# Third-stage products reordered, sums and stores of h moved forward, the first raw weights loaded by GpSimd's queue

## The chip, the cores and the metric

The kernel runs on one core of a Trainium2 chip. A core has five engines that run their own instruction streams and meet at semaphores: TensorE (PE, and PEld for its weight loads), VectorE (DVE), ScalarE (ACT), GpSimd (POOL) and SyncE (SP). DMA transfers are issued by SP's and GpSimd's queues here. The metric is the time of one execution on the device in microseconds (us).

## The reference

Sigmoid attention, then a "max of three" layer, then a layer with PReLU, all in float32:

```python
scores = scale * q @ k.T - log(S)          # 4 x 12 heads, S = 448, width 64
x = (1 / (1 + exp(-scores))) @ v           # -> 1792 tokens x 768
h = maximum(maximum(x @ w1, x @ w2), x @ w3)   # 768 x 768 each
x = h @ w_out                              # 768 x 768
h2 = x @ w_in                              # 768 x 2048
g = maximum(h2, 0) + alpha * minimum(h2, 0)
return g @ w_out2                          # 2048 x 768
```

## The kernel before

**Products.** Every matrix product behind attention is done by seven products for a 2 x 2 block (Strassen's scheme). A *unit* `u` is a pair of 128-wide column blocks of a weight matrix; for each unit there are seven products `k` = 0..6 for each of two halves `g` of the tokens. A product is nine matmuls of 128 x 448 columns: three slices of the contraction, and three for each, since a float32 operand is cut into a high half `h` (a cast on ScalarE, L277) and a low half `l` (source minus high half, on VectorE, L281), and low x high, high x low and high x high are added up.

**Banks.** `product(u, k, g)` (L831) writes three PSUM banks: k = 0 starts `X`, and ScalarE copies it to `V` (L850), to which k = 1 adds; k = 2 starts `W`; k = 3 and 4 add to `X`, and after each ScalarE copies `X` out (L865); k = 5 finishes `X`, k = 6 finishes `W`. The eviction (`evict`, L786) adds the copies to `W` on VectorE (`tensor_op`, L288). A product that adds to `X` while the copy of `X` still runs has to wait for it, and k = 1 waits for the copy to `V`.

**Stages.** Attention (0 to 138 us): scores L542, values L563, with q and k loaded by SP (L523), v by GpSimd (L531). Units 0 to 8 make h: three units, for w1, w2 and w3, for each of three column pairs, with the maximum on VectorE (`mx`). Behind the third unit `h_store` (L757) makes the sums that the next layer's seven products need (T = B12 - B11, then B22 - T and so on, into the same tiles) and GpSimd stores them to `hd` (L767); `reload` (L885) brings them back and cuts them. The *third stage* is h @ w_out: units 100 to 105, with g the half and weights `cf` from `cd` (`left_loads`, L942). Units 9 to 16 make the PReLU layer, behind which `ff3` follows (to the end).

**Weights.** A raw word `z` (384 KB) is loaded to `wr` by `load_half` (L132, four buffers; 112 words) on SP; `word_ops` (L230) unpacks it (two ScalarE passes, three VectorE instructions: L249, L250, L258); `unit_ops` (L314) adds and subtracts words (`wu`, `wt`) and cuts the seven left operands `f{u}_{k}`, from words 0 and 1 for k = 0 and 1, from all four for k = 2, 3 and 6. For w_out the operands are stored (L351) for the third stage; the words of units 9 and 10 are stored (`words_via`) and loaded as `wb`.

**Order.** All this is put by a planner into the programs while TensorE's products are written out by hand: `op(engine, columns, fn, *deps, gate, soon, lag)` registers a piece of work; each `advance()` behind a product emits what is ready and what fits a budget of columns, the `soon` ones first; `lag=n` holds an op back by n further steps behind what it depends on; `need()` forces out what a product is about to read. Each engine then works in the order in which its instructions were emitted, and so waits at the first that is not ready. The third stage's order is the loop behind `units(0, L, ...)`: for each of six units k = 0 to 6. L is 8, HK is 3, CU is 100, ND0 is 9.

## Time and profile before

| | us |
|---|---|
| median of three runs (955.11 to 958.52) | 958.07 |
| the profiled execution | 953.27 |
| its span in the trace | 951.5 |
| TensorE busy in the span | 873.8 |
| VectorE, ScalarE, GpSimd busy | 654.7, 525.8, 140.6 |

The mean granted TensorE clock over the span is 0.974 of full speed. The shares are averages over stages of different kinds. Where TensorE is the engine that is almost always busy, one looks at its pauses: an instruction's row carries, in brackets, the idle time before it and the instruction that ended it.

### The profile page before, as it was taken

Reading aid. Unit: us, or ns where it says so; the run is one execution under the profiler, and the core shown is the slowest. Engines: PE = TensorE matmul, PEld = TensorE weight load, DVE = VectorE, ACT = ScalarE, POOL = GpSimd, SP = SyncE. Lnnn points to the kernel's source line nnn. Section 1 sums busy time; section 2 is a strip of 40 time slices with the busy share of each in tenths; the row PEclk is TensorE's granted clock in tenths of the full one; section 3 lists DMA queues with packets and bytes.
Section 4 is the critical chain, followed back from the end, with each engine's and each line's share of the span. In section 5 each row is a group of like instructions: output and inputs, shape, how many; then the busy total and the mean of one; then the engine's idle time right before and its main releaser. Section 6 shows DMA issues by size and latency. Waiting matters only on the chain.

```text
span 951.5 us, 14131 instructions
## 1 busy us (share of the span) xinstructions
PE 873.8 (92%) x4878; PEld 742.0 (78%) x4878; DVE 654.7 (69%) x1289; ACT 525.8 (55%) x1021; POOL 140.6 (15%) x260
## 2 busy tenths in 40 slices
PE   9999997799699879988886789989999999999998
PEld 4466446698589778877775679888899999999997
DVE  1766766578588768777535459877886868787741
ACT  6877885444355536454424457765665755354530
POOL 1333000002210221320000013122222100000110
PEclk9999999899899979999998989999999999999999
DMA  7899520246544747697530126664544699834511
GB/s 241 293 306 308 161 72 6 85 143 206 174 139 143 230 150 221 240 352 223 178 112 26 47 72 197 205 223 143 174 147 165 230 348 374 301 106 152 175 50 48
DMA packets 78632, 170.46 MB, mean 179 GB/s; under 512 B 11120, under 2 KB 51856, under 8 KB 78560
## 3 DMA queue, kind: packets, MB, share of 16 engines
q1 hardware_dynamic: 61776, 111.10, 37.7%
q0 software_dynamic: 16496, 58.11, 16.4%
q8 instruction: 38, 0.62, 0.3%
q10 hardware_dynamic: 288, 0.34, 0.1%
q14 instruction: 34, 0.28, 0.1%
HBM read 123.12 MB, written 46.40 MB: 178 GB/s over the span
## 4 chain that ended last, share of the span: by engine, by line
PE 82%; DVE 7%; issue 4%; ACT 3%; DMA 3%; POOL 1%; SPq 0%; DVEq 0%; ACTq 0%; POOLq 0%
PE u_0X L670 15%; PE u_1X L670 13%; PE eW L670 9%; PE eX L670 9%; PE u_0W L670 8%; PE u_1W L670 6%; PE sc L542 6%; PE pav L563 6%; PE u_0V L670 4%; PE u_1V L670 3%; PE eV L670 3%; DMA qt<-in_q_dram 2%; ACT u L865 1%; DVE mx L288 1%; DVE wr L250 1%
## 5 line engine op out<-in xcount | busy, mean ns | idle before, releaser
L542 PE MATMUL sc<-qt,kt 64*64 64x448 f32 x672 | 97.6, 540 | 4.8 <-DMA qt<-in_q_dram 4.8
L563 PE MATMUL pav<-a,vt 64*64 64x448 f32 x672 | 95.9, 538 | 0.0
L550 ACT ACTIVATE a<-sc,bias_s 128x896 f32<-128x896 f32 x84 | 83.2, 1011 | 21.2 <-PE sc L542 20.2
L542 PEld LDWEIGHTS sc<-qt,kt 64*64 64x64 f32 x672 | 42.4, 134 | 36.4 <-issue 26.6
L258 DVE CUSTOM_DVE_ANT_0 wt<-wr,wt 128x768 uint16<-128x768 uint16 x112 | 62.6, 558 | 3.9
L250 DVE SCALAR_TENSOR_TENSOR wr<-wr 128x384 uint32<-128x384 uint32 x112 | 62.0, 553 | 3.4 <-ACT wr L242 3.1
L242 ACT ACTIVATE wr<-wr 128x384 uint32<-128x384 uint32 x112 | 61.6, 551 | 0.0
L865 ACT COPY u<-u_0X 128x448 f32<-128x448 f32 x40 | 21.3, 533 | 71.7 <-PE u_0X L670 71.7
L563 PEld LDWEIGHTS pav<-a,vt 64*64 64x64 f32 x672 | 40.1, 133 | 26.7 <-issue 20.8
L239 ACT ACTIVATE wt<-wr 128x384 f32<-128x384 f32 x100 | 55.3, 553 | 1.4 <-DMA wr<-in_weights_dram 1.4
L717 DVE SCALAR_TENSOR_TENSOR r<-n,nalpha,r 128x448 f32<-128x448 f32 x64 | 42.6, 681 | 16.9 <-ACT n L714 16.8
L750 POOL DMA_DIRECT2D gd<-r x48 | 26.3, 549 | 167.8 <-DVE r L717 148.8
L288 DVE TENSOR_TENSOR u<-u_1W,u 128x448 f32<-128x448 f32 x34 | 21.2, 624 | 37.9 <-ACT u L865 27.5
L288 DVE TENSOR_TENSOR u<-u_0W,u 128x448 f32<-128x448 f32 x34 | 21.2, 623 | 37.2 <-ACT u L865 34.6
L938 POOL DMA_DIRECT2D wd<-wt x32 | 17.8, 556 | 194.6 <-DVE wt L258 184.1
L865 ACT COPY u<-u_1X 128x448 f32<-128x448 f32 x40 | 21.3, 534 | 43.3 <-PE u_1X L670 43.3
L249 DVE TENSOR_SCALAR wt<-wt 128x384 uint32<-128x384 uint32 x112 | 39.8, 355 | 1.4 <-ACT wt L239 1.0
L578 DVE COPY x<-pav 128x448 f32<-128x448 f32 x12 | 7.5, 625 | 38.0 <-PE pav L563 38.0
L670 PE MATMUL u_0W<-x_2h,f_2l 128*128 128x448 f32 x27 | 12.1, 447 | 21.9 <-DVE f_2l L281 21.9
L850 ACT COPY u_0V<-u_0X 128x448 f32<-128x448 f32 x20 | 10.4, 518 | 38.1 <-PE u_0X L670 38.1
L670 PEld LDWEIGHTS u_0W<-x_2h,f_2l 128*128 128x128 f32 x27 | 5.8, 216 | 24.6 <-DVE f_2l L281 24.1
L1265 ACT COPY p<-eW 128x448 f32<-128x448 f32 x12 | 6.4, 534 | 32.9 <-PE eW L670 32.9
(813 smaller groups left out, 2828.1 us busy)
## 6 DMA issues: line engine op xcount, KB each, us to landing
wr<-in_weights_dram SPq DMA_DIRECT2D x112, 384.0 KB, 3.7
gl<-gd SPq DMA_DIRECT2D x79, 224.0 KB, 4.0
wl<-wd SPq DMA_DIRECT2D x64, 192.0 KB, 4.5
gd<-r POOLq DMA_DIRECT2D x48, 224.0 KB, 3.0
gl_T<-gdT SPq DMA_DIRECT2D x32, 224.0 KB, 5.3
hr<-hd POOLq DMA_DIRECT2D x28, 224.0 KB, 5.9
wd<-wt POOLq DMA_DIRECT2D x32, 192.0 KB, 3.9
kt<-in_k_dram SPq DMA_DIRECT2D x23, 224.0 KB, 4.8
```

What stands on the lines that cost most here:

```text
L239: nc.scalar.activation(st["T"].bitcast(F32), st["r"][:, :, 1].bitcast(F32), AF.Abs, scale=2.0**-112)
L242: nc.scalar.activation(st["r"][:, :, 0], st["r"][:, :, 0], AF.Copy, scale=2.0**-29)
L249: nc.vector.tensor_scalar(st["T"], st["T"], 3, None, ALU.logical_shift_left)
L250: nc.vector.scalar_tensor_tensor(out=st["r"][:, :, 0], in0=st["r"][:, :, 1], scalar=0x80000000, in1=st["r"][:, :, 0], op0=ALU.bitwise_and, ...
L258: nc.vector.tensor_tensor(out=st["T"], in0=st["r"][:, :, 0], in1=st["T"], op=ALU.add)
L288: nc.vector.tensor_tensor(out=out, in0=a, in1=b, op=op)
L542: nc.tensor.matmul(sc[g * KH : (g + 1) * KH, j, :S], keys[u, z][r, m * KH : (m + 1) * KH], queries[u, z][r], start=True, stop=True,)
L550: nc.scalar.activation(a, sc[:, :, :S], AF.Sigmoid, bias=bias_s, scale=scale)
L563: nc.tensor.matmul(pv[key][j * D : (j + 1) * D, :S], vts[u][r, m, j], a[r, j], start=start, stop=stop,)
L670: nc.tensor.matmul(ps[:, : rh.shape[-1]], lt, rh, start=(start and z == 0), stop=(stop and z == len(mms) - 1), skip_group_check=True,)
L717: nc.vector.scalar_tensor_tensor(out=s["r"], in0=s["n"], scalar=nalpha[:, f : f + 1], in1=s["r"], op0=ALU.mult, op1=ALU.add,)
L865: nc.scalar.copy(side[g, k], banks[X][:, :TW])
```

## The change

- **Attention.** Raw words z < 16 are loaded by GpSimd's queue instead of SP's. The first unit's words are registered with pair 4 instead of pair 7, behind a gate that waits until all w_out pieces are cut. The stores of those pieces come two steps later.
- **`h_store`.** Stores get `lag=2` and `soon`, the four sums get `soon` and lose their lag; so a store stands three steps or more behind its sum, an overwrite of T at the next step behind its store.
- **Reload.** The lag moves from the cut to the load (which has nothing that it depends on), and the tiles come in the order 0, 2, 3, 1, 4, 6, 5.
- **Third stage.** Each unit's products run in the order 0, 2, 3, 1, 4, then product 0 of the next unit, then 6 and 5; the copies are kept by unit so that two units can be open. The end of unit 8 is drawn together with it (its last two products stand behind the first two of unit 100), and product 0 of unit 9 stands in front of the last two of unit 105. `left_loads` follows this list.
- **Passage to unit 9.** Its words are registered at the second product of unit 104 instead of the start of unit 105, without a gate on the words; only the pieces 4 to 6 keep gates.

```diff
@@ -133,7 +133,8 @@
         if z >= NZ:
             return
         t = wpool.tile([P, HF, 2], U32, tag="wr", name=f"wr{z}", bufs=4)
-        nc.sync.dma_start(out=t.rearrange("p f t -> p (f t)"), in_=weights[z])
+        queue = nc.gpsimd if z < 16 else nc.sync
+        queue.dma_start(out=t.rearrange("p f t -> p (f t)"), in_=weights[z])
...
-                op("Q", 0, gone, op("Q", 0, put, o), lag=2)
+                op("Q", 0, gone, op("Q", 0, put, o, lag=2))
...
-                        unit_ops(-1 - r, zc[r], words=lambda z: word_ops(z, early=True), store=True)
+                        done += unit_ops(-1 - r, zc[r], words=lambda z: word_ops(z, early=True), store=True)
...
-                if (u, c) == (7, 0):
-                    unit_ops(0, zu[0])
+                if (u, c) == (4, 0):
+                    free_ws = lambda: all(o.step is not None for o in done)
+                    unit_ops(0, zu[0], words=lambda z: word_ops(z, gate=free_ws))
...
-                return op("Q", 0, store, *deps)
+                return op("Q", 0, store, *deps, lag=2, soon=True)
...
-            o1 = op("D", TW, t1)
+            o1 = op("D", TW, t1, soon=True)
             p1 = put(2, lambda: b["T"], o1)
-            o3 = op("D", TW, lambda: tensor_op(B12, B22, B12, ALU.subtract), o1)
+            o3 = op("D", TW, lambda: tensor_op(B12, B22, B12, ALU.subtract), o1, soon=True)
             put(4, lambda: B12, o3)
-            o2 = op("D", TW, lambda: tensor_op(b["T"], B22, b["T"], ALU.subtract), p1, lag=2)
+            o2 = op("D", TW, lambda: tensor_op(b["T"], B22, b["T"], ALU.subtract), p1, soon=True)
             put(3, lambda: b["T"], o2)
-            o4 = op("D", TW, lambda: tensor_op(B21, B21, b["T"], ALU.subtract), o2, o21, lag=2)
+            o4 = op("D", TW, lambda: tensor_op(B21, B21, b["T"], ALU.subtract), o2, o21, soon=True)
             held[g] = [o22, put(5, lambda: B21, o4)]
...
-            X, V, W = ((g, x) for x in "XVW")
+            X, V, W = ((u, g, x) for x in "XVW")
...
-            o = op("Q", 0, load, gate=lambda: homes_h(c, 3) and gate())
-            o = split_ops(
-                hf[g, c, r], make, lambda: st["x"], TW, o, gate=lambda: homes_h(c, 2), lag=2
-            )
+            o = op("Q", 0, load, gate=lambda: homes_h(c, 3) and gate(), lag=2)
+            o = split_ops(hf[g, c, r], make, lambda: st["x"], TW, o, gate=lambda: homes_h(c, 2))
...
-            for x in o:
+            for x in o[skip:]:
...
+            for n, (p, k) in enumerate(third):
+                f, d = wf[CU + p][k], cd[-1 - p % HK, k]
+                if n < 3:
+                    gate = lambda: all(o.step is not None for o in last) and (L, 0, 0) in made
+                elif n < 5:
+                    gate = lambda n=n: (L, (0, 2)[n - 3], 1) in made
+                else:
+                    gate = lambda x=third[n - 4]: (CU + x[0], x[1], x[0] // HK) in made
...
-                for c in range(7):
+                for c in inner:
...
+        inner = (0, 2, 3, 1, 4, 6, 5)
+        third = [(0, 0)]
+        for p in range(2 * HK):
+            third += [(p, k) for k in inner[1:5]] + [(p + 1, 0)] * (p < 2 * HK - 1) + [(p, k) for k in inner[5:]]
         first, seq = (0, 2, 1, 3, 4, 5, 6), (0, 2, 3, 4, 1, 5, 6)
         units(0, L, first, range(7), (
-            (0, 0), (0, 1), (2, 0), (1, 0), (3, 0), (1, 1), (4, 0), (2, 1), (5, 0), (6, 0), (3, 1),
-            (4, 1), (5, 1),
+            (0, 0), (0, 1), (2, 0), (3, 0), (2, 1), (1, 0), (4, 0), (3, 1), (6, 0), (5, 0), (1, 1), (4, 1),
         ))
 
-        back = {}
-        for n in range(2 * HK):
-            g, r = n // HK, n % HK
-            u = CU + n
+        z0, z1 = zu[ND0], zu[ND0 + 1]
+        extra = {0: (L, 6, 1), 1: (L, 5, 1), len(third) - 3: (ND0, first[0], 0)}
+        for n, (p, k) in enumerate(third):
+            u = CU + p
             if n == 0:
-                for c in range(4):
+                for c in inner[:4]:
                     for x in range(HK - 1):
-                        reload(1, c, x, lambda: (L, 6, 1) in made)
-            elif n == HK - 1:
-                for c in range(4, 7):
+                        reload(1, c, x, lambda: (L, 5, 1) in made)
+            elif (p, k) == (HK - 1, inner[1]):
+                for c in inner[4:]:
                     for x in range(HK - 1):
                         reload(1, c, x, lambda: True)
-            elif n == 2 * HK - 1:
-                z, at = zu[ND0], {0: 0, 1: 0, 2: 3, 3: 4, 4: 5, 5: 6, 6: 6}
+            elif (p, k) == (2 * HK - 2, inner[1]):
+                at = {4: 1, 5: 4, 6: 6}
                 cuts = unit_ops(
-                    ND0, z, [lambda k=k: (u, at[k], 1) in made for k in range(7)],
-                    words=lambda x: via[0][x - z](lambda: (u - 1, 5, 1) in made),
+                    ND0, z0, [lambda k=k: k not in at or (CU + 2 * HK - 1, at[k], 1) in made for k in range(7)],
+                    words=lambda x: via[0][x - z0](None),
                 )
-            for k in range(7):
-                product(u, k, g)
-                advance(STEP)
-                if (n, k) == (0, 0):
-                    step(L, 6, 1)
-        z1 = zu[ND0 + 1]
+            product(u, k, p // HK)
+            advance(STEP)
+            if n in extra:
+                step(*extra[n])
         unit_ops(
             ND0 + 1, z1, None,
             words=lambda x: via[1][x - z1](lambda: all(o.step is not None for o in cuts)),
@@ -1022,7 +1021,7 @@
 
         units(ND0, ND1 - 1, first, seq, (
             (0, 1), (0, 0), (2, 1), (3, 1), (2, 0), (4, 1), (1, 1), (3, 0), (5, 1), (6, 1),
-        ))
+        ), 1)
         swap()
 
         advance(STEP)

```

Where the diff leaves open what the planner makes of it, the programs' orders show it. First VectorE in unit 3, where the first `h_store` falls: `h00_t` and `h10_t` are the two halves' T, `mx` the maxima, `f3_1l` and `f3_2l` the low halves that products 1 and 2 of unit 3 read; the lines L249, L250, L258 (after: L250, L251, L259) are one word. Before:

```order
L258 ISA wt36_2468<-wr36_2395,wt36_2468 128x768
L288 TENSOR_TENSOR wu3_2544<-wt34_2430,wt35_2448 128x384
L288 TENSOR_TENSOR h00_t_2562<-mx0_0_1_1879,mx0_0_0_1739 128x448
L288 TENSOR_TENSOR h00_t_2562<-mx0_1_1_1802,h00_t_2562 128x448
L288 TENSOR_TENSOR mx0_1_0_1842<-mx0_1_0_1842,h00_t_2562 128x448
L288 TENSOR_TENSOR h10_t_2583<-mx0_0_3_2018,mx0_0_2_1859 128x448
L288 TENSOR_TENSOR h10_t_2583<-mx0_1_3_1942,h10_t_2583 128x448
L288 TENSOR_TENSOR mx0_1_2_1981<-mx0_1_2_1981,h10_t_2583 128x448
L281 TENSOR_TENSOR f3_2l_2593<-wu3_2544,f3_2h_2572 128x384
L288 TENSOR_TENSOR wt34_2430<-wt32_2356,wt34_2430 128x384
```

After:

```order
L289 TENSOR_TENSOR h00_t_2494<-mx0_0_1_1874,mx0_0_0_1733 128x448
L289 TENSOR_TENSOR mx0_0_1_1874<-mx0_1_1_1796,mx0_0_1_1874 128x448
L289 TENSOR_TENSOR h10_t_2517<-mx0_0_3_2012,mx0_0_2_1856 128x448
L289 TENSOR_TENSOR mx0_0_3_2012<-mx0_1_3_1936,mx0_0_3_2012 128x448
L282 TENSOR_TENSOR f3_1l_2536<-wt33_2408,f3_1h_2478 128x384
L250 TENSOR_SCALAR wt34_2426<-wt34_2426 128x384
L251 SCALAR_TENSOR_TENSOR wr34_2342<-wr34_2342 128x384
L259 ISA wt34_2426<-wr34_2342,wt34_2426 128x768
L289 TENSOR_TENSOR h00_t_2494<-mx0_1_1_1796,h00_t_2494 128x448
L289 TENSOR_TENSOR mx0_1_0_1836<-mx0_1_0_1836,h00_t_2494 128x448
L289 TENSOR_TENSOR h10_t_2517<-mx0_1_3_1936,h10_t_2517 128x448
L289 TENSOR_TENSOR mx0_1_2_1978<-mx0_1_2_1978,h10_t_2517 128x448
```

The first sums of both T now stand ahead of `f3_1l`, with other sums, `f3_1l` and a word between each of them and the instruction that overwrites it. Behind these rows another word, `wu3` and `f3_2l` follow, so the overwrites still stand ahead of `f3_2l`.

Second TensorE in the third stage, unit 101, at the end of product 3 (weights `cf1_3`). Before:

```order
L670 MATMUL u101_0X_4385<-h0_31h_4099,cf1_30_4375 128x448
L670 MATMUL u101_0X_4385<-h0_3h_4223,cf1_31_4377 128x448
L670 MATMUL u101_0X_4385<-h0_3l_4255,cf1_30_4375 128x448
L670 MATMUL u101_0X_4385<-h0_3h_4223,cf1_30_4375 128x448
L670 MATMUL u101_0X_4385<-h0_40h_4101,cf1_41_4399 128x448
L670 MATMUL u101_0X_4385<-h0_40l_4285,cf1_40_4397 128x448
L670 MATMUL u101_0X_4385<-h0_41h_4117,cf1_41_4399 128x448
```

After:

```order
L672 MATMUL u101_0X_4322<-h0_31h_4086,cf1_30_4336 128x448
L672 MATMUL u101_0X_4322<-h0_3h_4211,cf1_31_4338 128x448
L672 MATMUL u101_0X_4322<-h0_3l_4231,cf1_30_4336 128x448
L672 MATMUL u101_0X_4322<-h0_3h_4211,cf1_30_4336 128x448
L672 MATMUL u101_0V_4332<-h0_10h_4104,cf1_11_4360 128x448
L672 MATMUL u101_0V_4332<-h0_10l_4277,cf1_10_4358 128x448
L672 MATMUL u101_0V_4332<-h0_11h_4106,cf1_11_4360 128x448
```

Behind the product that ends in `X`, before, the next one adds to `X` again; after, it adds to `V`.

Third ScalarE at the start of unit 9: casts of the weight pieces `f9_k` and the copy of unit 9's product 0 to bank V (`u9_0V`). Before:

```order
L277 CAST f9_0h_5118<-wb68_4987 128x384
L850 COPY u9_0V_5132<-u9_0X_5122 128x448
L277 CAST f9_1h_5138<-wb69_4989 128x384
L277 CAST f9_2h_5140<-wu9_5059 128x384
L277 CAST f9_5h_5157<-wb71_4993 128x384
L277 CAST y12_0h_5159<-y12_11_5004 128x448
L277 CAST y12_1h_5161<-y12_21_5089 128x448
L713 ACTIVATE r0_0_5174<-u9_0V_5132 128x448
L714 ACTIVATE n0_0_5175<-u9_0V_5132 128x448
L277 CAST y11_3h_5178<-y11_t_4960 128x448
L277 CAST f9_3h_5183<-wb68_4987 128x384
L865 COPY u9_0_3_5196<-u9_0X_5122 128x448
```

After:

```order
L278 CAST f9_0h_4933<-wb68_4879 128x384
L278 CAST f9_1h_4935<-wb69_4881 128x384
L852 COPY u105_1V_4949<-u105_1X_4939 128x448
L278 CAST y02_2h_4955<-y02_t_4828 128x448
L278 CAST y02_4h_4957<-u102_0_3_4591 128x448
L278 CAST f9_2h_4982<-wu9_4937 128x384
L803 COPY y11_21_4994<-u104_1X_4812 128x448
L278 CAST y10_0h_5001<-y10_11_4776 128x448
L278 CAST f9_3h_5005<-wb68_4879 128x384
```

The casts of pieces 0 to 3 have moved ahead of the copy `u9_0V`, which follows 11 instructions behind the last of these rows, with the casts of pieces 4 to 6 right behind it.

## Rows read from the trace of the kernel before

**Rows 1.** The page: busy us, share of the span and instructions of each engine.

```profile
PE 873.8 (92%) x4878; PEld 742.0 (78%) x4878; DVE 654.7 (69%) x1289; ACT 525.8 (55%) x1021; POOL 140.6 (15%) x260
```

**Rows 2.** Waits of PE in 200:413, 413:506, 504:562: total us, times, longest.

```profile
PE u_0W L670 <- DVE f_2l L281: 19.7, 4, 8.8
PE u_1X L670 <- ACT u L865: 1.2, 2, 0.6
...
PE u_1X L670 <- ACT u L865: 3.7, 6, 0.6
PE u_1V L670 <- ACT u_1V L850: 1.8, 3, 0.6
...
PE u_0W L670 <- DVE f_2l L281: 5.9, 2, 3.9
PE u_0X L670 <- DVE f_0l L281: 4.8, 2, 2.6
```

**Rows 3.** Attention: PE's wait, SP's issue (start, us), the chain (start, us).

```profile
PE sc L542 <- DMA qt<-in_q_dram: 4.8, 3, 2.1
...
52.43 2.07 SPq L136 DMA_DIRECT2D wr<-in_weights_dram  x2
...
54.55 5.80 DMA qt<-in_q_dram
```

**Rows 4.** Timeline of PE, third stage: start us, us, instruction [idle before <-releaser].

```profile
423.04 0.47 PE L670 MATMUL u_0X<-h_40h,cf 128*128 128x448 f32 x1 [0.62 <-ACT u L865]
425.75 0.47 PE L670 MATMUL u_0X<-h_50h,cf 128*128 128x448 f32 x1 [0.62 <-ACT u L865]
...
438.43 0.47 PE L670 MATMUL u_0X<-h_40h,cf 128*128 128x448 f32 x1 [0.62 <-ACT u L865]
```

**Rows 5.** Timelines of DVE and PE at the first h store, unit 3.

```profile
244.28 0.62 DVE L288 TENSOR_TENSOR h_t<-mx,h_t 128x448 f32<-128x448 f32 x1 [4.06 <-DMA hd<-h_t]
...
248.93 0.63 DVE L288 TENSOR_TENSOR h_t<-mx,h_t 128x448 f32<-128x448 f32 x1 [2.83 <-DMA hd<-h_t]
...
250.74 0.74 PE L670 MATMUL u_0W<-x_2h,f_2l 128*128 128x448 f32 x1 [8.70 <-DVE f_2l L281]
...
254.14 0.37 PE L670 MATMUL u_1W<-x_2h,f_2l 128*128 128x448 f32 x1
```

**Rows 6.** Timeline of DVE: a word's steps, and sums one behind the other.

```profile
237.81 0.35 DVE L249 TENSOR_SCALAR wt<-wt 128x384 uint32<-128x384 uint32 x1
...
239.14 0.55 DVE L288 TENSOR_TENSOR wu<-wt,wt 128x384 f32<-128x384 f32 x1
...
503.21 0.61 DVE L288 TENSOR_TENSOR y_t<-u,y_t 128x448 f32<-128x448 f32 x1
503.74 0.62 DVE L281 TENSOR_TENSOR y_4l<-u,y_4h 128x448 fp32r<-128x448 f32 x1
```

**Rows 7.** Windows: busy PE, PEld, DVE, ACT, POOL; clock; DMA share, GB/s; DMA issues.

```profile
408.00:432.00 24.00, 21.21 (x99) 18.18 (x99) 18.23 (x34) 13.46 (x29) 2.89 (x6) 1.00 0.98 353
456.00:480.00 24.00, 21.02 (x99) 18.20 (x100) 15.07 (x27) 10.25 (x21) 0.00 (x0) 1.00 0.57 180
504.00:528.00 24.00, 15.56 (x63) 12.78 (x62) 12.26 (x23) 9.29 (x20) 0.55 (x1) 0.86 0.14 44
...
hr<-hd POOLq DMA_DIRECT2D x23, 224.0 KB, 6.1
...
cf<-cd-1_0l SPq DMA_DIRECT2D x1, 192.0 KB, 9.9
```

**Rows 8.** Timelines of PE and DVE at the start of units 9, 10 and 12.

```profile
508.84 0.47 PE L670 MATMUL u_0X<-y_0h,f_0l 128*128 128x448 f32 x1 [2.25 <-DVE f_0l L281]
...
513.06 0.56 DVE L281 TENSOR_TENSOR f_2l<-wu,f_2h 128x384 fp32r<-128x384 f32 x1 [3.21 <-ACT f_2h L277]
...
552.81 0.74 PE L670 MATMUL u_0W<-y_2h,f_2l 128*128 128x448 f32 x1 [3.88 <-DVE f_2l L281]
...
614.09 0.47 PE L670 MATMUL u_0W<-y_2h,f_2l 128*128 128x448 f32 x1 [2.33 <-DVE f_2l L281]
```

More of the change, by code (lines that the diff above doesn't have):

```diff
@@ L504, in attention @@
         nu = n // 2
-        keys, queries, vts, at, pv = {}, {}, {}, {}, {}
+        keys, queries, vts, at, pv, done = {}, {}, {}, {}, {}, []
         def halves(u, c):
@@ L942, in left_loads, with load @@
         def left_loads():
-            n = 0
             for p in range(2 * HK):
                 wf[CU + p] = [{} for _ in range(7)]
-                for k in range(7):
-                    f, d = wf[CU + p][k], cd[-1 - p % HK, k]
-                    if n < 3:
-                        gate = lambda: all(o.step is not None for o in last) and (L, 0, 0) in made
-                    elif n < 5:
-                        gate = lambda n=n: (L, n - 3, 1) in made
-                    else:
-                        gate = lambda p=(n - 4) // 7, k=(n - 4) % 7: (CU + p, k, p // HK) in made
-                    def load(f=f, d=d, nm=f"cf{p}_{k}"):
-                        for x in range(2):
-                            f[x] = wslot(f"{nm}{x}", F32R)
-                            nc.sync.dma_start(out=f[x].bitcast(F32), in_=d[x])
-                    maker[id(f)] = op("Q", 0, load, gate=gate)
-                    n += 1
+            for n, (p, k) in enumerate(third):
[6 more added lines that the diff above has]
+                    gate = lambda x=third[n - 4]: (CU + x[0], x[1], x[0] // HK) in made
+                def load(f=f, d=d, nm=f"cf{p}_{k}"):
+                    for x in range(2):
+                        f[x] = wslot(f"{nm}{x}", F32R)
+                        nc.sync.dma_start(out=f[x].bitcast(F32), in_=d[x])
+                maker[id(f)] = op("Q", 0, load, gate=gate)
         def begin(u):
```

11 lines of the change are left out of this document (5 added, 6 removed).

## The prediction

> **What bounds the kernel now.** I read the engines' shares first: TensorE is busy 873.8 us of the 951.5 us span [rows 1], and behind 710 us the view of waits lists no pause of it, so the time to be won is TensorE's pauses before that. Next come TensorE's waits stage by stage [rows 2]: in each row the reader looks at the releaser and at the total. 200 to 413 us: 19.7 us on VectorE's `f_2l`, in only four pauses, the longest 8.8. 413 to 506 us, the third stage: pauses of 0.6 us, six for each token half on a ScalarE copy of the `X` bank (one half's row is shown), and five on a copy into the `V` bank (three in the row shown), 17 in all. 504 to 562 us: 5.9 us on `f_2l`, 4.8 on `f_0l`, and three smaller releasers. In attention 4.8 us, on three loads of `qt` [rows 3]. So no engine but TensorE is full; what counts is the order in which VectorE, ScalarE and the queues meet its products.
>
> A pause costs more than its length. In [rows 4] one product and one pause take 425.75 − 423.04 = 2.71 us, and seven products with three pauses 438.43 − 423.04 = 15.39 us. Hence a product is (15.39 − 3 × 2.71) / 4 = 1.815 us, and a pause shown as 0.62 costs 0.895 us: 0.27 us more than it shows. After the longest pauses the next product is slow too: from 250.74 to 254.14 us 3.40 us pass for 1.815 [rows 5], which is 1.6 us more.
>
> **Third stage, reordered: −16 us.** The ordered products X3, X4, X5 write one bank and wait for its copy each time; V1 behind X0 waits likewise. In the new order another bank's product stands between any two. W6, whose sum needs the copy of X4, has one product, 1.815 us, in front of it. The copy is what the pause of 0.62 waited for, a sum's step is 0.54 (503.74 − 503.21 [rows 6]), together 1.2, so the cover holds by 0.6 us. 17 pauses × 0.895 = 15.2; two more stand in the last unit of the stage before [rows 2] and cost 1.8, but its new tail has pauses of its own (below). I take 16 together. The weights of a product (384 KB in two loads) are now wanted every 1.8 instead of 2.2 us; the stretch 456 to 480 us moved 180 GB/s at a DMA share of 0.57 [rows 7], so 1.22 times that fits.
>
> **Passage to the second MoE, words registered a unit earlier: −18 us.** From X0 of unit 9 to W2 of unit 10, 552.81 − 508.84 = 43.97 us pass for 13 products worth 23.6; with the pause in front of X0 (2.25) and the slow product behind the last pause (1.6), 24.2 us are lost. VectorE is not busy there: its `f_2l` waits 3.21 us for ScalarE's `f_2h` [rows 8]. That cast stands in ScalarE's order behind the copy `u_0V`, which waits for product X0. So each product waits for a copy, a cast and a low half that start when the product before it ends. In the new order the casts f9_0h to f9_3h stand before that copy; f9_4h to f9_6h stand some products ahead of use. Left over, summing the steps along the new order from the product that each chain starts at, less the products in between (0.54 for a sum or a low half on VectorE [rows 6], some 0.45 for a copy or a cast on ScalarE and 0.1 for each handover, estimates from the 0.62 of a copy's pause): 0.75 on y12_0l, 1.64 on y12_2 and 0.54 on f10_0l behind late sums, and 1.9 on f10_2l, which stands behind the sum with the copied X4. That is 4.8 us in five pauses, 6.2 with the 0.27 each. So 24.2 − 6.2 = 18.
>
> As a test, the same sums along the order of before give 2.4 us for the first pause of this stretch and 4.2 for the last; the trace shows 2.25 and 3.88 [rows 8]. They leave out DMA and the clock.
>
> **The two h stores: −13 us, and other units +16.** Before, the overwrites of T wait 4.06 and 2.83 us for T's stores, with `f_2l` behind them on VectorE [rows 5]: TensorE stands still 8.7 us. In the changed order T's sums stand ahead of `f3_1l`, and two sums, a low half and a word (0.54 + 0.54 + 0.47 + 1.33 = 2.9 us; the word is 239.14 − 237.81 [rows 6], 0.47 an estimate for 384 columns from 0.54 for 448) and the other half's sum (0.54) stand between a T and its overwrite: 3.4 us. Since the store lands 2.8 to 4.1 us after the sum, some 0.5 us of wait remains. But VectorE still does this work in front of `f3_2l`: the sums from u2_1W's end to `f3_2l` give pauses of 0.3, 2.9 and 0.4 us in unit 3, 2.6 in unit 6. With 0.5 us of store each and 0.27 a pause, 5.0 and 3.4 us instead of 8.7 + 0.27 + 1.6 = 10.6 each: −12.8.
>
> What it costs: the same registering and `soon` sums put one word or two sums more in front of the other units' low halves. Summed likewise: unit 2, 1.8 (f2_0l behind unit 1's last sums), 2.55 and 0.4; unit 4, 1.4 and 2.7; unit 5, 1.3 and 0.5; unit 7, 2.2; unit 8, 3.05, 0.4 and 1.2. That is 17.5 us in 11 pauses, 20.5 with their restarts. Before, these units had the two other `f_2l` pauses of [rows 2] (19.7 − 17.5 = 2.2) and small ones on `f_3l`, some 4.7 with restarts. Net +15.8.
>
> **Start of the third stage: +10 us.** The last unit's tail is drawn together, so unit 100's first low halves come right behind the last sums: h0_00l stands behind the sum with the copy of u8's X4 (2.3 us), h0_20l behind two sums and a subtraction (2.2), h0_30l (2.2), h0_60l (0.5), h0_50l (1.15): 8.4 us in five pauses, 9.7 with restarts. Before, this place shows no pause on a low half. Nothing in the trace shows this order, so the bounds: 4 us if half of the low halves come in time, 13 if the clock is lowered here as at 504 us (0.86 [rows 7]).
>
> **562 to 710 us: −2.5 us.** The first of three `f_2l` pauses, 2.33 at 614.09 us [rows 8], goes in the new order (the unit's words no longer stand there); the other two stay as they are.
>
> **Raw weights on GpSimd's queue: −4 us.** On SP a `wr` load that waits for its buffer holds back the k and q behind it; one pair of `wr` took 2.07 us at 52.43, and the `qt` behind it, issued at 54.55, landed 5.80 us later, TensorE waiting for it [rows 3]. Without the `wr` they are issued when their own buffers are free. I take 4.0 of the 4.8. On GpSimd's queue the 16 loads now stand behind `vt` loads that wait for attention; behind them wait the word work on ScalarE and VectorE and the stores of its pieces, none of which TensorE needs before 138 us. Bounds: −5 and, if the first words of unit 0 came late, +2.
>
> The Trainium skill ("DMA: Bandwidth & Descriptors", section "Issuing engines are not separate DMA queues") says that transfers started by different engines run on the same 16 DMA engines and interleave, and that another issuing engine saves only the time to initiate. By that rule this term is near zero; the row on SP's wait shows an issue held back by a buffer, on which the rule is silent.
>
> **DMA in the denser third stage: +1 us** (0 to 6). The first weights are now registered some 7.3 us of products ahead of use, before 13; a load took up to 9.9 us, and an h reload 6.1 us, while the share was 0.98 [rows 7]. The reloads of g = 0, which filled that stretch, are issued earlier than they were, so I stay near the low end.
>
> **Sum.** −16 − 18 − 12.8 + 15.8 + 10 − 2.5 − 4 + 1 = −26.5 us. Against the profiled execution's 953.3 that is 926.8. The median of the runs is 958.1, 4.8 above the profiled one; with the same distance, 931.6. The uncounted remainder of lower clock at the passage points a little further down; I say **930 us**. What a measurement can tell from no change is 0.5%, 4.8 us.
>
> **Rivals.**
> 1. *The loads become the wait.* If the first weights and the h reloads of g = 1 land in 10 us as at 400 us, three weights come 2 to 3 us late and ScalarE, which casts the h tiles in order, holds its bank copies back: +8, 938 us. For: the shorter lead and the share of 0.98. Against: no wait for a DMA on TensorE there before. Chance 0.15.
> 2. *The queue changes nothing*: the three waits on `qt` stay because the bytes share the DMA engines: +4, 934 us. For: 5.80 us for a `qt` of 224 KB is near the 6.1 of an h reload of that size at the share of 0.98 [rows 3, 7], so the bytes themselves were slow. Against: the late `qt` is the one behind two `wr` in its own queue. Chance 0.17. The rule of the Trainium skill named above would end here.
> 3. *The stores don't get out of the way.* The change's words name overwrites three steps behind their stores; the code puts the stores three steps behind their sums and takes the overwrites' delay away. If GpSimd issues T's store as late as before, VectorE waits 4.06 and 2.83 again at both stores: +13 with the slow products, 943 us. Chance 0.08.
> 4. *Slower, by the clock.* Where pauses of 2 to 4 us stood before every second product or so, the granted clock was 0.86 [rows 7, 8]. The new order spreads pauses of 1.3 to 3 us over units 2 to 100. If the clock were 0.86 from 200 to 560 us, some 290 us of products at full clock would take 1/0.86 − 1 = 16% longer, +47: 977 us. It decides from about 0.91 down (+29, 959 us). Against: in units 4 to 7 two or three pauses in 14 products, not one before each. Chance 0.04.
> The forecast itself, 920 to 938, has 0.50; better than that (the start of the third stage without its pauses), 0.06.
>
> **How the numbers follow.** Range: the forecast's bounds, widened to rivals 1 to 3 and to the lower bound of the start (−6) and of the passage (−5): 916 to 946; outside are rival 4 and part of the tails. Faster by over 0.5% means under 953.3: all but rival 4 and an adding up of 1 and 3: 0.92. Within 0.5% 0.04, slower 0.04.
>
> **What would show it.** Right: in the third stage a unit takes 12.7 us instead of 15.39 and no waits on `u` copies; at 500 to 560 us no VectorE wait for an `f` cast over 1 us; at 240 us a pause near 3 instead of 8.7; new pauses on `f_2l` and `f_0l` of 1.3 to 3 us in units 2, 4, 7 and 8, and on low halves of `h` at 400 to 415. Wrong: TensorE waiting for `cf` or for ScalarE's h casts, a granted clock under 0.95 over units 2 to 8, or a store wait on VectorE above 2 us.

## The result and the profile after

The changed kernel takes **931.5 us** (median of four runs, 928.7 to 932.6); the kernel before, beside it on the same chip, 957.2. The ratio is 0.9729, 95% interval 0.9700 to 0.9758. The prediction said 930 and 916 to 946; this is its likeliest case. The profiled execution took 928.7 us, where the sum of the prediction's terms gave 926.8 (that its span is 926.8 too is chance: the span before was 951.5 for an execution of 953.3). So −24.6 us were measured for a sum of −26.5, and the misses of the terms partly cancel.

The page of after, engines' busy time as in [rows 1]:

```profile
PE 869.6 (94%) x4878; PEld 765.1 (83%) x4878; DVE 654.3 (71%) x1289; ACT 527.8 (57%) x1021; POOL 148.5 (16%) x276
```

TensorE's waits of the changed kernel, in 138:200, 200:413, 413:506 and 504:562 us (columns: us in total, times, longest), answer to [rows 2]:

```profile
PE u_0V L672 <- DVE f_1l L282: 4.3, 1, 4.3
PE u_0X L672 <- DVE f_0l L282: 3.8, 1, 3.8
...
PE u_0W L672 <- DVE f_2l L282: 17.4, 7, 3.3
PE u_0X L672 <- DVE f_0l L282: 3.3, 2, 1.9
PE u_0W L672 <- DVE f_6l L282: 1.1, 1, 1.1
...
PE u_0X L672 <- DVE h_00l L282: 2.3, 1, 2.3
PE u_0W L672 <- DVE h_20l L282: 2.2, 1, 2.2
PE u_0X L672 <- DVE h_30l L282: 2.1, 1, 2.1
...
PE u_0W L672 <- DVE f_2l L282: 1.7, 1, 1.7
PE u_1W L672 <- DVE y_2l L282: 0.9, 1, 0.9
```

In the third stage the waits on bank copies are gone and the three new ones on `h` low halves are 2.3, 2.2 and 2.1 us, as summed along the new order (2.3, 2.2, 2.2). In units 2 to 8 the four `f_2l` pauses, two of them near 8.8 us, have become seven of at most 3.3 us. At the passage (504 to 562 us) 3.7 us are left in all, of 16.7 before. No row of TensorE names a DMA in these windows.

The windows of after (columns as in [rows 7]):

```profile
240.00:264.00 24.00, 20.42 (x93) 18.19 (x92) 15.96 (x34) 10.16 (x21) 4.40 (x9) 0.93 0.49 155
...
456.00:480.00 24.00, 24.00 (x121) 22.24 (x120) 20.06 (x38) 14.54 (x30) 0.00 (x0) 1.00 0.71 220
...
504.00:528.00 24.00, 21.93 (x104) 18.96 (x103) 20.07 (x38) 15.31 (x33) 2.17 (x4) 1.00 0.21 72
```

456 to 480 us is full: TensorE busy 24.00 of 24.00, and the weights come at 220 GB/s, 1.22 times the 180 of before. At 504 us the clock is 1.00 instead of 0.86. At 240 us, behind the first h store, it is 0.93 in a window whose two timelines (VectorE, then TensorE) answer to [rows 5]:

```profile
242.01 0.62 DVE L289 TENSOR_TENSOR h_t<-mx,h_t 128x448 f32<-128x448 f32 x1
...
243.21 0.62 DVE L289 TENSOR_TENSOR h_t<-mx,h_t 128x448 f32<-128x448 f32 x1
...
247.06 0.56 DVE L282 TENSOR_TENSOR f_2l<-wu,f_2h 128x384 fp32r<-128x384 f32 x1 [0.58 <-ACT f_2h L278]
```

```profile
247.68 0.74 PE L672 MATMUL u_0W<-x_2h,f_2l 128*128 128x448 f32 x1 [2.89 <-DVE f_2l L282]
248.21 0.57 PE L672 MATMUL u_0W<-x_2l,f_2h 128*128 128x448 f32 x1
248.59 0.57 PE L672 MATMUL u_0W<-x_2h,f_2l 128*128 128x448 f32 x1
...
251.36 0.37 PE L672 MATMUL u_1W<-x_2l,f_2h 128*128 128x448 f32 x1
251.56 0.36 PE L672 MATMUL u_1W<-x_2h,f_2l 128*128 128x448 f32 x1
```

Neither overwrite of T waits any more here (at the second h store, in unit 6, one waits 0.24 us instead of 3.70). TensorE's pause is 2.89 us instead of 8.70. Behind it matmuls start 0.38 us apart (248.21, 248.59) and later 0.20 (251.36, 251.56): the granted clock is 0.50 from 247.70 to 251.10 us and 1.00 from 251.20 to 254.00, the two levels of 1.2 and 2.4 GHz.

**Where the time went.** Lay the products of a trace on a grid of 1.8155 us from unit 0's first one; what the starts run behind the grid is lost time. In after unit 3 starts at 236.42 us and unit 4 at 269.10, so 269.10 − 236.42 − 14 × 1.8155 = 7.26 us are lost between them. A pause in front of a unit's first product is counted with that unit, as the prediction did: of the 7.26 us, 1.49 go with the pause on unit 4's `f_0l`, and 2.11 us go likewise with unit 2's (the two `f_0l` pauses, 3.3 us, in the second window above). By place, before and after, with the forecast:

| place | before | after | difference | forecast |
|---|---|---|---|---|
| start of unit 0's first product | 137.86 | 132.94 | −4.9 | −4 |
| units 0, 1 | 19.0 | 21.7 | **+2.7** | 0 |
| units 3, 6 (the h stores) | 21.8 | 11.0 | −10.8 | −12.8 |
| units 2, 4, 5, 7, 8 | 5.6 | 22.1 | +16.5 | +15.8 |
| copies in the third stage and unit 8's end | 17.1 | 0.1 | −17 | −16 |
| start of the third stage, DMA | 0 | 11.3 | +11.3 | +10 + 1 |
| passage, units 9 and 10 | 25.2 | 5.4 | −19.8 | −18 |
| unit 12 | 2.7 | 0.1 | −2.6 | −2.5 |

Copies and pauses on `h` in unit 8's last products (1.8 before, 2.5 after) are counted with the third stage, the 2.25 us in front of unit 9 [rows 8] with the passage. These add up to −24.6; the spans differ by 24.7. Lost time is read from one profiled execution of each kernel, and a difference of 2 or 3 us in it can be the clock of that execution.

### The profile page after: what moved, and what is told of

Read it like the earlier page. It is cut to its first block, busy times and chain, and to the rows that moved or that the text cites. A ratio compares the mean times of both kernels' runs of the same rounds, so it can differ in the third digit from the quotient of the medians.

```text
span 926.8 us, 14153 instructions
## 1 busy us (share of the span) xinstructions
PE 869.6 (94%) x4878; PEld 765.1 (83%) x4878; DVE 654.3 (71%) x1289; ACT 527.8 (57%) x1021; POOL 148.5 (16%) x276
## 4 chain that ended last, share of the span: by engine, by line
PE 85%; DVE 11%; issue 2%; ACT 2%; DMA 0%; POOL 0%; DVEq 0%; ACTq 0%; POOLq 0%
PE u_0X L672 15%; PE u_1X L672 13%; PE eW L672 9%; PE eX L672 9%; PE u_0W L672 7%; PE sc L543 7%; PE pav L564 7%; PE u_1W L672 7%; PE u_0V L672 4%; PE u_1V L672 3%; PE eV L672 3%; DVE mx L289 2%; DVE wr L251 1%; DVE u L289 1%; DVE wt L259 1%
## 5 line engine op out<-in xcount | busy, mean ns | idle before, releaser
L543 PE MATMUL sc<-qt,kt 64*64 64x448 f32 x672 | 108.2, 541 | 0.1
L564 PE MATMUL pav<-a,vt 64*64 64x448 f32 x672 | 106.8, 537 | 0.0
L543 PEld LDWEIGHTS sc<-qt,kt 64*64 64x64 f32 x672 | 55.7, 134 | 21.0 <-issue 12.9
L259 DVE CUSTOM_DVE_ANT_0 wt<-wr,wt 128x768 uint16<-128x768 uint16 x112 | 62.6, 559 | 3.9
L564 PEld LDWEIGHTS pav<-a,vt 64*64 64x64 f32 x672 | 54.0, 132 | 13.6 <-issue 7.8
L251 DVE SCALAR_TENSOR_TENSOR wr<-wr 128x384 uint32<-128x384 uint32 x112 | 61.9, 553 | 3.7 <-ACT wr L243 3.1
L719 DVE SCALAR_TENSOR_TENSOR r<-n,nalpha,r 128x448 f32<-128x448 f32 x64 | 42.9, 682 | 11.3 <-ACT n L716 10.8
L938 POOL DMA_DIRECT2D wd<-wt x32 | 17.4, 544 | 197.6 <-DVE wt L259 186.8
L250 DVE TENSOR_SCALAR wt<-wt 128x384 uint32<-128x384 uint32 x112 | 40.1, 358 | 3.5 <-ACT wt L240 3.0
```

The source lines that it names most:

```text
L250: nc.vector.tensor_scalar(st["T"], st["T"], 3, None, ALU.logical_shift_left)
L251: nc.vector.scalar_tensor_tensor(out=st["r"][:, :, 0], in0=st["r"][:, :, 1], scalar=0x80000000, in1=st["r"][:, :, 0], op0=ALU.bitwise_and, ...
L259: nc.vector.tensor_tensor(out=st["T"], in0=st["r"][:, :, 0], in1=st["T"], op=ALU.add)
L543: nc.tensor.matmul(sc[g * KH : (g + 1) * KH, j, :S], keys[u, z][r, m * KH : (m + 1) * KH], queries[u, z][r], start=True, stop=True,)
L564: nc.tensor.matmul(pv[key][j * D : (j + 1) * D, :S], vts[u][r, m, j], a[r, j], start=start, stop=stop,)
L719: nc.vector.scalar_tensor_tensor(out=s["r"], in0=s["n"], scalar=nalpha[:, f : f + 1], in1=s["r"], op0=ALU.mult, op1=ALU.add,)
```

## The experiments

Eleven kernels. Ratios are to the kernel before on the same chip; "lost" is the time over the grid from unit 0 on, "sums" the pauses that the steps' durations, summed along a kernel's order, give without DMA or clock.

| kernel | median us | ratio, 95% | lost | sums |
|---|---|---|---|---|
| before | 957.2 | 1 | 97.8 | 61.2 |
| changed | 931.5 | 0.9729 (0.9700–0.9758) | 78.0 | 55.8 |
| e1_unit0_late | 906.5 | 0.9488 (0.9457–0.9520) | 56.2 | 40.0 |
| e2_h_store_old | 937.3 | 0.9802 (0.9771–0.9833) | 87.0 | 48.9 |
| e3_passage_late | 962.1 | 1.0078 (1.0051–1.0106) | 111.3 | |
| e4_third_order_old | 944.3 | 0.9866 (0.9824–0.9908) | 95.8 | 66.6 |
| a_wr_on_sp | 935.2 | 0.9799 (0.9773–0.9826) | 81.3 | |
| b_unit0_early | 982.8 | 1.0312 (1.0270–1.0355) | 127.0 | 81.6 |
| b_step_1800 | 929.2 | 0.9732 (0.9691–0.9774) | 74.7 | 37.2 |
| a_step_1800 | 875.1 | 0.9171 (0.9146–0.9195) | 25.7 | 13.4 |
| late_step_1700 | 880.1 | 0.9235 (0.9188–0.9283) | 30.1 | 20.3 |
| late_step_1800 | **856.2** | 0.8980 (0.8953–0.9007) | 5.9 | 1.6 |
| late_step_1800_h_old | 869.0 | 0.9107 (0.9077–0.9138) | 20.4 | 1.6 |

### One part undone at a time

**Unit 0's words registered late again:**

```diff
-                if (u, c) == (4, 0):
-                    free_ws = lambda: all(o.step is not None for o in done)
-                    unit_ops(0, zu[0], words=lambda z: word_ops(z, gate=free_ws))
+                if (u, c) == (7, 0):
+                    unit_ops(0, zu[0])
```

> The changed kernel with one part undone: unit 0's words are registered with pair 7 again, without the gate. Theory: this part alone moved VectorE's word work by one word against the products in units 2 to 8, and with it the pauses that the forecast put down as +16 and half of the +10. Summing VectorE's and ScalarE's steps along the order of this kernel gives 24 pauses of 40.0 us between 138 and 710 us, against 31 of 55.8 for the changed kernel: 15.8 us and some 2 us of restarts less, so 913 to 916 us; no pause on f_0l in units 2 and 4, f_2l pauses of about 1.3 in units 2, 4, 5 and 7 instead of 2.3, 2.6, 1.2 and 2.1, and none on h_00l at the start of the third stage. Rival 1: the pauses come from the h sums that are emitted first, and unit 0's early words matter nothing: 931. Rival 2: the early registration spares a wait at unit 0, so without it 933 to 936.

Measured 906.5 us, faster than any expectation. TensorE's waits in 200:413 us (this kernel runs some 20 us ahead, so two `h` rows fall in):

```profile
PE u_0W L671 <- DVE f_2l L282: 11.4, 7, 3.1
PE u_0W L671 <- DVE f_6l L282: 2.4, 1, 2.4
PE u_0W L671 <- DVE h_20l L282: 2.2, 1, 2.2
PE u_0X L671 <- DVE h_30l L282: 2.1, 1, 2.1
```

The `f_2l` pauses are shorter (11.4 us in all, not 17.4), and those on `f_0l` and `h_00l` are gone. So one part of the change, to which the prediction gave no term of its own, costs 0.9729 − 0.9488 = 0.024 of 957, 23 us. They lie in many places: units 2, 4, 5, 7 and 8 lose 14.2 us instead of 22.1, units 3 and 6 lose 6.5 instead of 11.0, and the start of the third stage 6.9 instead of 11.3. In the first and the last of these places more is still lost than before the change (5.6 and 0), though unit 0's words come late here as there.

**The old `h_store`** (no `lag` and `soon` on the stores and sums; the overwrites' own `lag=2` back):

```diff
-                return op("Q", 0, store, *deps, lag=2, soon=True)
+                return op("Q", 0, store, *deps)
...
-            o2 = op("D", TW, lambda: tensor_op(b["T"], B22, b["T"], ALU.subtract), p1, soon=True)
+            o2 = op("D", TW, lambda: tensor_op(b["T"], B22, b["T"], ALU.subtract), p1, lag=2)
```

> The changed kernel with h_store as it was before: stores without lag, sums not emitted first, overwrites with lag. Forecast's step: the h stores' change is worth 12.8 us, as VectorE's waits of 4.1 and 2.8 us for the stores go from both places. Summing the steps along this order, the pauses without DMA are 48.9 us against 55.8; if the waits for the stores return in full (13.8 us and two slow products, 3.2) the time is 931.5 - 6.9 + 17 - 1 = 940 to 942 us, with pauses of 8 us and more on f_2l in units 3 and 6. Rival (the stores were never the matter; the order of the sums is): 924 to 926 us and no DVE wait for hd<-h_t above 1 us.

Measured 937.3 us, a little under the theory. The overwrites' waits are back, with `f_2l` behind them (VectorE, then TensorE, unit 3):

```profile
246.06 0.62 DVE L289 TENSOR_TENSOR h_t<-mx,h_t 128x448 f32<-128x448 f32 x1 [4.16 <-DMA hd<-h_t]
...
251.32 0.63 DVE L289 TENSOR_TENSOR h_t<-mx,h_t 128x448 f32<-128x448 f32 x1 [3.44 <-DMA hd<-h_t]
...
253.66 0.56 DVE L282 TENSOR_TENSOR f_2l<-wu,f_2h 128x384 fp32r<-128x384 f32 x1 [0.58 <-ACT f_2h L278]
```

```profile
254.27 0.74 PE L672 MATMUL u_0W<-x_2h,f_2l 128*128 128x448 f32 x1 [11.42 <-DVE f_2l L282]
```

Units 3 and 6 lose 28.4 us, not 11.0: here the new stores save 17, more than forecast. But units 2, 4, 5, 7 and 8 lose 20.2 us instead of 22.1, so the h sums explain less than 2 us of what the prediction put under their heading.

**The passage registered late again** (unit 9's words at unit 105's first new product, with their gates, and unit 9's product 0 behind unit 105):

```diff
-            elif (p, k) == (2 * HK - 2, inner[1]):
-                at = {4: 1, 5: 4, 6: 6}
+            elif (p, k) == (2 * HK - 1, inner[1]):
+                at = {0: 0, 1: 0, 2: 3, 3: 4, 4: 5, 5: 6, 6: 6}
```

> The changed kernel with unit 9's words registered at the start of unit 105 again, with the old gates, and product 0 of unit 9 back behind the last of unit 105. Theory: each product of the passage then waits again for a copy, a cast and a low half; the sums along the order give pauses of 21.0 us in units 9 and 10 against 4.9, and 9.7 against 4.2 in units 12 to 14, in all 23 us more, and 3 to 5 us for the lower clock there (0.86 to 0.91 before): 956 to 960 us, granted clock under 0.95 in the stretch of unit 9. By the forecast's term of 18 alone: 949.5. Rival (it was the denser third stage that freed VectorE, not the registering): under 935.

Measured 962.1 us, above the theory and 0.8% slower than the kernel before. TensorE's busy time (first number behind the 24.00) and the clock in two windows:

```profile
504.00:528.00 24.00, 15.30 (x60) 12.54 (x60) 10.73 (x21) 9.12 (x20) 0.54 (x1) 0.86 0.14 44
528.00:552.00 24.00, 15.73 (x57) 12.99 (x57) 11.28 (x21) 9.94 (x21) 1.62 (x3) 0.86 0.08 29
```

The old passage is back, with the 0.86 of [rows 7]. The passage loses 31 instead of 5.4 us, and units 12 and 13 lose 13.4 instead of 5.0. The part is worth 1.0078 − 0.9729 = 0.035 of 957, 33 us, in the new order, not 18: its term was measured against the old one.

**The old product order in the third stage** (and the old tail of unit 8):

```diff
-        inner = (0, 2, 3, 1, 4, 6, 5)
+        inner = tuple(range(7))
```

> The changed kernel with the third stage's products in the old order 0 to 6 and the old tail of unit 8, the registering of unit 9's words kept at its new time. Theory: three pauses of 0.62 us per unit return (0.9 us each from start to start, 15 of them) and at the start of the third stage other pauses take the place of those on h_00l, h_20l and h_30l; along the order 66.6 us of pauses against 55.8, and 3 us of restarts: 944 to 946 us, unit period 15.4 us. By the forecast's two terms (-16 and +10): 937.5. Rival (the denser stage costs as much in late loads as it wins): 930 to 933.

Measured 944.3 us. TensorE's waits in 410:520 us:

```profile
PE u_1X L672 <- ACT u L867: 4.4, 7, 0.6
PE u_0X L672 <- ACT u L867: 3.7, 6, 0.6
PE u_0V L672 <- DVE h_10l L282: 2.2, 1, 2.2
PE u_0X L672 <- DVE h_00l L282: 2.1, 1, 2.1
...
PE u_0X L672 <- DVE h_50l L282: 1.3, 1, 1.3
```

The 0.6 us waits on copies return; the third stage loses 11 us more than in the changed kernel and unit 8 5 more. There are pauses on `h` low halves with the old order and the old tail too, so these are not needed to make them. That is why undoing this part costs 13 us, and not the 6 of the forecast's two terms (−16 and +10) together.

**Raw weights on SP's queue again:**

```diff
-        queue = nc.gpsimd if z < 16 else nc.sync
-        queue.dma_start(out=t.rearrange("p f t -> p (f t)"), in_=weights[z])
+        nc.sync.dma_start(out=t.rearrange("p f t -> p (f t)"), in_=weights[z])
```

> The changed kernel with every raw weight on SP's queue again; all else as changed. My reason (a wr load that waits for its buffer holds back the k and q behind it in SP's queue): TensorE waits for qt come back, some 4 to 5 us in all, the first product of unit 0 starts near 137 to 138 us instead of 132.9, and the time is 935 to 937 us. Rival, from the rule that issuing engines share the same DMA engines: the first product of unit 0 starts near 133 us and the time stays at 931 to 932. A third: unit 0's words are registered at pair 4 here, so more wr stand ahead of the q loads than in the kernel before, and more than 5 us are lost in attention: 938 to 945.

Measured 935.2 us, as the first theory had it; its interval (0.9773 to 0.9826) lies above that of the changed kernel. The first product of unit 0 in before, after and this kernel:

```profile
137.86 0.47 PE L670 MATMUL u_0X<-x_0h,f_0l 128*128 128x448 f32 x1
...
132.94 0.47 PE L672 MATMUL u_0X<-x_0h,f_0l 128*128 128x448 f32 x1
...
136.44 0.47 PE L671 MATMUL u_0X<-x_0h,f_0l 128*128 128x448 f32 x1
```

Of all thirteen kernels, the four with the loads on SP's queue start unit 0 at 136.2 to 137.9 us, the nine with GpSimd's at 131.2 to 133.8. The waits on `qt` return here (2.9 us, two) and TensorE has none in after. The mechanism shows in what SP's own queue waits for up to 138 us in this kernel: `wr` issues (L136) wait for VectorE to be done with a buffer, 16 times in all (in after 5 times).

```profile
SPq L136 <- DVE wt L258: 99.0, 16, 42.2
```

The k and q loads stand behind them in that queue. In GpSimd's timeline of after such a wait stands in front of a store of a piece instead (the `vt` loads stand in that queue too, and TensorE names none of them).

```profile
53.30 0.55 POOL L137 DMA_DIRECT2D wr<-in_weights_dram  x1 [1.09 <-DVE wt L259]
53.84 0.54 POOL L352 DMA_DIRECT2D cd-2_0h<-f-2_0h  x1
```

The Trainium skill ("DMA: Bandwidth & Descriptors", "Issuing engines are not separate DMA queues") says that another issuing engine saves only the time to initiate a transfer; by that rule alone this part would come to nothing. The runs show 3.5 us at the first product: what the other queue saves here is the wait for a buffer in front of the k and q loads, of which the rule says nothing. The lost time behind the first product is 3.2 us higher than in the changed kernel with nearly the same pauses on TensorE; the mean granted clock of this execution is 0.978 instead of 0.983.

### The early registration by itself

**The kernel before with that part alone** (the expectation names the two-step delay of the pieces' stores as well; the kernel that ran leaves that delay out, so only the registering and its gate differ from the kernel before):

```diff
-                if (u, c) == (7, 0):
-                    unit_ops(0, zu[0])
+                if (u, c) == (4, 0):
+                    free_ws = lambda: all(o.step is not None for o in done)
+                    unit_ops(0, zu[0], words=lambda z: word_ops(z, gate=free_ws))
```

> The kernel before, with one part of the change alone: unit 0's words registered at pair 4 behind the gate, and the two-step delay of the pieces' stores. Theory after the first runs (the early registration of unit 0 shifts which VectorE work stands ahead of which low half in all later units): the rows' steps summed along its order give 81.6 us of TensorE pauses where the order before gives 61.2, so about 20 us slower than before, 974 to 980 us, with the added pauses in units 0 to 8 and in the third stage. Rival, the prediction's own attribution (the added pauses of units 2, 4, 5, 7 and 8 come from the h stores' sums set in front): no change, 952 to 958 us.

Measured 982.8 us, 28 us slower than before and above the theory's range. Units 0 and 1 lose 21.7 us (19.0 before, 21.7 in the changed kernel) and units 2, 4, 5, 7 and 8 lose 16.4 more than before: nearly the two rises of the changed kernel, +2.7 and +16.5, without its h sums. The timelines of VectorE and TensorE at unit 3 show what the earlier registration does to the order:

```profile
252.11 0.63 DVE L288 TENSOR_TENSOR h_t<-mx,h_t 128x448 f32<-128x448 f32 x1 [4.33 <-DMA hd<-h_t]
...
257.98 0.63 DVE L288 TENSOR_TENSOR h_t<-mx,h_t 128x448 f32<-128x448 f32 x1 [4.05 <-DMA hd<-h_t]
...
259.19 0.55 DVE L288 TENSOR_TENSOR wu<-wt,wt 128x384 f32<-128x384 f32 x1
...
260.31 0.56 DVE L281 TENSOR_TENSOR f_2l<-wu,f_2h 128x384 fp32r<-128x384 f32 x1 [0.58 <-ACT f_2h L277]
```

```profile
260.93 0.74 PE L671 MATMUL u_0W<-x_2h,f_2l 128*128 128x448 f32 x1 [12.19 <-DVE f_2l L281]
```

Before, `wu` stood ahead of the overwrites (239.14 us [rows 6], 244.28 and 248.93 [rows 5]). Here it stands behind both, and the cast and the low half behind it. TensorE's pause there is 12.19 us. The sums gave +20; that the waits for stores grow (4.33 and 4.05 us for 4.06 and 2.83) is not in them.

### The planner's budget

VectorE is busy only 71% of the span, so the next theory was that the pauses that are left come from the order. One number of the planner is how many columns it may emit behind a product:

```diff
-    STEP = 1700
+    STEP = 1800
```

> The changed kernel with one number of the planner changed: the columns that may be emitted behind a product, 1800 instead of 1700. Theory (the pauses that are left are low halves that the planner emits a product too late, or behind a sum of the same step, and no engine is full): the sums along its order give 13.4 us of pauses instead of 55.8, so some 42 us go, 885 to 895 us. Rival 1 (VectorE's amount of work in units 1 to 8 makes the pauses, not its order): 925 to 932. Rival 2 (work that is emitted earlier finds buffers and loads not ready, DMA waits take the place): 900 to 915 with VectorE, ScalarE or TensorE waits on wr, hr or cf.

Measured 875.1 us, below the theory's range: what the sums leave out (restarts, slow products, the clock) went as well. All that TensorE still waits for on VectorE's low halves of `f`:

```profile
PE u_0W L672 <- DVE f_2l L282: 4.0, 2, 2.2
PE u_0X L672 <- DVE f_0l L282: 3.0, 1, 3.0
PE u_0V L672 <- DVE f_1l L282: 1.8, 1, 1.8
```

Rival 1 falls by the time. The waits that rival 2 named are there on ScalarE (from 138 to 700 us 9.5 us in six waits for `wr`, the longest 4.2, and up to 1.4 on an `hr`), but TensorE has no pause on a DMA or on the `h` low halves, and the time is 25 us under that rival's range: here they cost little.

The same number in the kernel before:

> The kernel before with 1800 columns a step instead of 1700 and nothing else. The sums along its order give 37.2 us of pauses instead of 61.2, none of them on low halves in units 2 to 7; 13 of the 37 are copies of the banks in the third stage, 12 the passage to units 9 and 10. Theory: 24 us less by the sums, and up to 17 more if the overwrites' waits for the stores of T no longer stand ahead of the low half for product 2: 914 to 930 us. Rival: the stores' waits stay in front of a low half as before (8.7 and 8.8 us pauses), 928 to 934. What is then left against the changed kernel at 1800 (875) is what the third stage's order, the passage and GpSimd's queue are worth, some 40 us.

Measured 929.2 us, the upper end. TensorE's waits in 200:420 us:

```profile
PE u_0X L670 <- DVE f_3l L281: 8.6, 1, 8.6
PE u_0X L670 <- ACT u L865: 6.8, 4, 3.5
```

The low halves of units 2 to 7 are on time but for one, behind the first h store: another than in [rows 5], `f_3l`, and the same 8.6 us. Pauses on ScalarE's copies, up to 3.5 us, are new beside the 0.6 of [rows 2]. VectorE still waits 4.51, 3.46, 5.37 and 4.03 us for the stores of T. The rival holds.

So at 1800 columns the change saves 929.2 − 875.1 = 54 us, at 1700 only 26. The difference of 28 us is what the order that 1700 columns make of the changed program gives back.

**Both**, unit 0's words registered with pair 6 and no gate, first with 1700 columns, then with 1800:

```diff
-                if (u, c) == (4, 0):
-                    free_ws = lambda: all(o.step is not None for o in done)
-                    unit_ops(0, zu[0], words=lambda z: word_ops(z, gate=free_ws))
+                if (u, c) == (6, 0):
+                    unit_ops(0, zu[0])
```

> The changed kernel with unit 0's words registered with pair 6 and no gate, 1700 columns as in the changed kernel. The sums along its order give 20.3 us of pauses against 1.6 at 1800 columns: 12 of them in units 9 to 14, 8 in units 0 to 8. Theory: 856 + 19 + some 5 for restarts and the clock, 874 to 884 us. Rival (with registration at pair 7 the time was 906, and registration one pair earlier matters little): 898 to 908.

> The changed kernel with both: unit 0's words registered with pair 6 and no gate, and 1800 columns a step. The sums along its order give 1.6 us of pauses. Theory: nearly all of what the first run without the early registration still lost (56 us over the product grid, some 10 of it not pauses) goes: 860 to 875 us. Rival 1 (DMA waits take the place, with hr, cf or wr loads whose lead is now 4 to 6 us): 880 to 895. Rival 2 (VectorE's amount of work decides): 900 to 908 as without the step change.

Measured 880.1 us, within its range, and 856.2 us (this one ran before the other), below its range. The second takes 0.898 of the time of before and 0.92 of the changed kernel's. One pair of attention (6 instead of 7 in e1) moves 26 us. The window 200:413 us of the last one:

```profile
200.00:413.00 213.00, 211.72 (x1042) 194.45 (x1042) 183.30 (x368) 121.81 (x254) 43.34 (x80) 1.00 0.72 235
```

TensorE works 211.72 of 213 us at full clock, with VectorE busy 183 of them (86%) and the DMA engines at 0.72: neither is the limit in this stretch.

**That kernel with the old `h_store`:**

> The fastest so far (unit 0 at pair 6, 1800 columns) with the sums and stores of h as in the kernel before. Here the low half for product 2 of units 3 and 6 stands ahead of the sums of h in both orders. Theory (a store's wait on VectorE costs only when a low half that TensorE wants next stands behind it): VectorE still waits several us for the stores, TensorE hardly, 856 to 862 us. Rival (the wait for the stores itself costs, as the 17 us it cost in the changed kernel): 870 to 876.

Measured 869.0 us, 13 more: between the two. The theory's condition was too narrow. No low half is late; ScalarE carries the wait on (VectorE, ScalarE and TensorE in unit 3):

```profile
230.94 0.63 DVE L289 TENSOR_TENSOR h_t<-mx,h_t 128x448 f32<-128x448 f32 x1 [4.12 <-DMA hd<-h_t]
```

```profile
235.13 0.51 ACT L278 CAST f_0h<-wt 128x384 fp32r<-128x384 f32 x1 [5.55 <-DVE wt L259]
235.54 0.52 ACT L866 COPY u<-u_1X 128x448 f32<-128x448 f32 x1
```

```profile
236.12 0.74 PE L671 MATMUL u_1X<-x_4h,f_4l 128*128 128x448 f32 x1 [3.99 <-ACT u L866]
```

The overwrite waits for the store, a word waits behind it on VectorE, a cast waits for the word on ScalarE, the copy of `X` stands behind the cast, and the product that adds to `X` waits for the copy. So a wait for a DMA on one engine reaches TensorE through another.

## Why the prediction came out, step by step

- **Third stage, −16.** Right (−17): the copies' waits are gone, and return in e4.
- **Start of the third stage, +10.** Right in size (11.3, the pauses at the places and lengths summed), wrong in cause. It was put to the drawn-together tail; but e4 has two of these pauses (`h_00l` and `h_50l`) with the old order and tail, and late_step_1700 and a_step_1800, with the new ones, have none. The early registration of unit 0 is not needed either: e1, without it, keeps two (2.2 and 2.1 us). What the runs agree with is that the pauses hang on the planner's phase, that is on which piece of work falls behind which product; which edit sets it here stays open.
- **Passage, −18, and unit 12, −2.5.** Right (−19.8, −2.6). That undoing the part costs 33 us once the rest is changed was not in the prediction.
- **h stores, −12.8.** Mis-sized: −10.8. The store waits went (0.24 us is left) and the pause of unit 3 came out as summed (2.89 for 2.9; unit 6's is 3.33 for 2.6), but what a pause costs beyond its length had been priced at 0.27 us. Behind 2.89 us the product takes 251.16 − 247.68 = 3.48 us for 1.82, 1.7 more, and behind 3.33 us 1.6 more, which the prediction gave to pauses of 8.7 only. Length alone does not decide it: behind a pause of 2.95 us in unit 8 the next product is not slow.
- **Other units, +15.8.** Size right (+16.5), cause wrong in the main. The prediction put it to the registering and the `soon` sums of the h stores. The kernel before with unit 0's early registration alone shows +16.4 as well; the old `h_store` in the changed kernel takes away less than 2. But the early registration is enough and not needed for all of it: e1, without it, still loses 8.6 us more here than before. Which of the other edits makes those stays open.
- **Units 0 and 1, no term.** The step that failed: the registration of unit 0 at pair 4 was described and given no term of its own. In units 0 and 1, +2.7 were lost (for one, the pause on `f_1l` is 4.3 us instead of 3.7); over the whole kernel the registration costs 23 us, most of it where the prediction had summed the pauses and named another cause.
- **Raw weights, −4.** Right: −4.9, and −3.5 by undoing it.
- **DMA, +1.** No DMA wait on TensorE: 0. The share in 384 to 408 us was 0.86, the rows of TensorE name no load, and ScalarE and VectorE wait for none from 400 to 445 us either.

**Rivals.** 1 (the loads become the wait) is refuted by the absence of any DMA in TensorE's waits, and in ScalarE's at the start of the third stage. 2 (the queue changes nothing) by 132.94 against 136.44. 3 (the stores stay in front) by the two `h_t` rows without a wait and the 0.24 us at the second store. 4 (the clock) was half there: 0.93 in several windows where the prediction set its sign at 0.95, but never 0.86 between 200 and 560 us; the mean over the span rose from 0.974 to 0.983.

The forecast was near because the sums along the order found nearly every pause, whatever made it: each place came out within 2.7 us of its term, so the total is not luck. What the sums can't do is say which edit made which pause. Runs with one edit alone or one undone help, but their differences do not add up: the early registration costs 28 us on the kernel before and 23 in the changed one, the passage 18 forecast and 33 undone.

What stays open: why the planner keeps the shifted phase for nine units after pair 4 was only followed in the orders, not in its budget step by step; and the extra 8 us of b_unit0_early over its sum were not split: units 3 and 6 lose 6.3 us more there than before, by pauses, stores and clock together.
